# Loads in the order of need, and five projection blocks ahead of the first output projection, in a sliding-attention and gated feed-forward layer

## The chip, the core and the metric

One core of one Trainium2 chip runs the whole layer in one launch. The metric is the device time of that launch in microseconds (us). The kernel before took 820.35 us, the median of seven runs (820.05 to 825.86, six of them within 820.05 to 820.52). An edit is judged by the ratio of its time to this kernel's on the same chip.

## What is computed

The input is x, 2048 rows of 1024 bf16 numbers. The layer adds a dilated sliding attention and then a gated feed-forward to it, each behind a layer norm.

```python
qkv = layernorm(x) @ wqkv                      # 1024 -> 3 x 1024, 32 heads of 32
off = arange(8) * 2                            # a row sees 8 rows: itself, 2, 4, ... 14 back
logits = einsum("bhsd,bhswd->bhsw", q, kg) * 32 ** -0.5
attn = softmax(where(mask, logits, -1e9))
h = x + einsum("bhsw,bhswd->bhsd", attn, vg) @ wo
g, u = layernorm(h) @ w_gate, layernorm(h) @ w_up      # 1024 -> 3584 each
out = h + (g * u) @ w_down
```

## The kernel before, in words

**Tiling.** The 2048 rows are worked in four chunks of 512. A chunk's normalized rows lie transposed in SBUF as lnT (three buffers), so that TensorE can use them as the moving operand. Weights stream through a pool of seven buffers of 1 MB, one for each block of 512 columns. The query-key-value projection of a chunk has six such blocks (two for queries, two for keys, two for values) of four groups of eight 128x512 matmuls; ScalarE evicts each group from PSUM (L249) and SP stores it to DRAM (L252 for queries, L261 for keys and values), from where Pool's DMAs fetch it back with heads and quarter-chunks on the partitions (L351, L352, L357), the layout in which VectorE does the attention. The result goes through DRAM again (L427, L430) into oT, for the output projection with wo, its residual add and the second layer norm (`wo_ln2`, L440 to L467). Then come the gate and up projections (`ffn1`) and the down projection (`ffn2`).

**Order of TensorE's work.** Chunk 0's projection, chunk 1's, chunk 2's, four blocks of chunk 3's, the output projection of chunk 0, the last two blocks of chunk 3's, and then for each chunk `ffn1`, the next chunk's `wo_ln2`, `ffn2` (L528 to L550). The first block of chunk 0 is a stage of its own, the opening: as each quarter of 128 rows arrives, VectorE takes its statistics and normalizes it, TensorE transposes it into PSUM (`first_transpose`, L285), ScalarE copies half of the transposed tile to SBUF and VectorE the other half (`first_copy`, L291), and TensorE multiplies it with block 0 of wqkv (`first_mm`, L294).

**Order of the rest.** The program order of every engine is written out by hand. `Background` (L33) holds generators: the first layer norm of chunks 1 to 3 (`ln1`, L188) and the attention of each chunk (`attention`, L364). After each group of matmuls `bg.step` lets them emit as much VectorE work as the group's 1.73 us pay for. An engine runs its instructions in that order, so where a wait stands in an engine's queue, all that was emitted later on it stands behind.

**The opening loads.** SP issues, in this order: quarters 0 and 1 of x, block 0 of wqkv in two halves, quarter 2, block 1 of wqkv in two halves, quarter 3 (L221, L213), and then with `pump` (L144) blocks 2 to 5 of wqkv and the first block of wo (L148). Pool copies one element of quarter 3 (L320), which makes it wait for that load, and then issues the loads of x for chunks 1 to 3 (L182). Each DMA that SP issues takes the next of eight semaphores, and waits until the DMA that used it before, eight places earlier, has landed.

**Buffers that tie stages together.** Eight buffers hold quarters of x or h, so the loads of chunk 2 wait for chunk 0's normalizing and those of chunk 3 for chunk 1's. Four buffers (`ln`) hold normalized quarters until their DMA transpose (L196, L447) has landed. PSUM has eight buffers, and 30 buffers (`t1k`) hold evicted groups.

Of the kernel before, what the change touches and what calls it, by code (L numbers as in the profile page):

```python
# [8 lines left out]
BF = mybir.dt.bfloat16  # L9
# [14 lines left out]
TC = 512  # L24
NCH = S // TC
SUB = TC // 4
KO = D // 128
# [48 lines left out]
def kernel(  # L76
# [11 lines left out]
    nc = tc.nc  # L88
# [50 lines left out]
        for b in range(4):  # L139
            stream.append((("wd", NCH - 1, hf, b), wd_v[:, bass.ts(b, 7), bass.ts(hf, 512)], 7))  # L140
    wts = {}
    state = {"next": 0, "live": 0}

    def pump(eng=None):  # L144
        while state["next"] < len(stream) and state["live"] < 7:
            key, src, n = stream[state["next"]]
            wt = wpool.tile([128, KO, 512], BF, tag="w", name="w_" + "_".join(map(str, key)))
            (eng or nc.sync).dma_start(wt[:, 0:n, :], src)  # L148
            wts[key] = wt
            state["next"] += 1  # L150
            state["live"] += 1

# [25 lines left out]
    def load_x(c, what, eng):  # L178
        tiles = []
        for t in range(4):  # L180
            xt = hp.tile([128, D], BF, tag="h", name=f"{what}{c}_{t}")
            eng.dma_start(xt[:], x[bass.ds(c * TC + t * 128, 128), :])  # L182
            tiles.append(xt)
        return tiles

    lnTs = {}

    def ln1(c):  # L188
        xts = load_x(c, "x", nc.gpsimd)
        yield "later", 8.0 if c < 3 else 5.0  # L190
        lnTs[c] = lnTp.tile([128, KO, TC], BF, tag="lnT", name=f"lnT1_{c}")
        mv4, rs4 = ln_tiles(f"1_{c}")

        def norm(t):
            ln = normalize(xts[t], mv4, rs4, t)
            nc.sync.dma_start_transpose(lnTs[c][:, :, bass.ts(t, 128)], ln[:])  # L196

        for t in range(4):
            stats(xts[t], mv4, t)
            rstd_of(mv4, rs4, t, t + 1)  # L200
            yield 1.5
            if t > 0:
                norm(t - 1)
                yield 0.55
        norm(3)
        yield 0.55


    def load_w(parts=1):
        key, src, n = stream[state["next"]]  # L210
        wt = wpool.tile([128, KO, 512], BF, tag="w", name="w_" + "_".join(map(str, key)))
        for q in range(parts):
            nc.sync.dma_start(wt[:, bass.ts(q, KO // parts), :], src[:, bass.ts(q, KO // parts), :])  # L213
        wts[key] = wt
        state["next"] += 1
        state["live"] += 1

    x0 = [hp.tile([128, D], BF, tag="h", name=f"x0_{t}") for t in range(4)]

    def load_x0(t):  # L220
        nc.sync.dma_start(x0[t][:], x[bass.ds(t * 128, 128), :])  # L221

    load_x0(0)
    load_x0(1)
    load_w(2)
    load_x0(2)
    load_w(2)
    load_x0(3)
    nc.scalar.preload_act_table_set("natural_log_exp_and_others")
    warm = const.tile([128, 512], BF)  # L230
# [52 lines left out]
        lns[t] = normalize(x0[t], mv0, rs0, t)  # L283

    def first_transpose(t):  # L285
        pts[t] = psum.tile([128, KO, 128], BF, tag="mm", name=f"pt{t}")
        for kk in range(KO):
            nc.tensor.transpose(pts[t][:, kk, :], lns[t][:, bass.ts(kk, 128)], ident[:])  # L288
        nc.scalar.copy(lnTs[0][:, 0:4, bass.ts(t, 128)], pts[t][:, 0:4, :])  # L289

    def first_copy(t):  # L291
        nc.vector.tensor_copy(lnTs[0][:, 4:8, bass.ts(t, 128)], pts[t][:, 4:8, :])  # L292

    def first_mm(t, kos):  # L294
        for ko in kos:
# [20 lines left out]
        if t < 3:  # L316
            first_rstd(t + 1)
    first_mm(3, range(8))
    order_after_x0 = const.tile([128, 1], BF)
    nc.gpsimd.tensor_copy(order_after_x0[:], x0[3][:, 0:1])  # L320
    pump()
    bg.add(ln1(1))
    bg.add(ln1(2))
    for j in range(4):
# [35 lines left out]
    def prefetch_qk(c):  # L360
        if c in stored and ("q", c) not in qkv_in:
            load_qk(c)

    def attention(c):  # L364
        if c == 0:
            load_qk(0)
            load_v(0)
            yield "later", 7.0
        qD, kD, vD = qkv_in["q", c], qkv_in["k", c], qkv_in["v", c]
        lg = att.tile([128, W, SUB], F32, tag="lg", name=f"lg{c}")  # L370
        for wp in range(W // 2):
            prod = att.tile([128, 2, DH, SUB], BF, tag="prod", name=f"prod{c}_{wp}")
            for j in range(2):
                o = HB - DIL * (2 * wp + j)
                nc.vector.tensor_tensor(prod[:, j], qD[:], kD[:, :, o:o + SUB], ALU.mult)  # L375
                yield 2.3
            nc.vector.tensor_tensor(prod[:, :, 0:16], prod[:, :, 0:16], prod[:, :, 16:32], ALU.add)  # L377
            yield 2.3
            nc.vector.tensor_tensor(prod[:, :, 0:8], prod[:, :, 0:8], prod[:, :, 8:16], ALU.add)
            yield 1.2  # L380
            t3 = att.tile([128, 2, 4, SUB], F32, tag="t3", name=f"t3{c}_{wp}")
            nc.vector.tensor_tensor(t3[:], prod[:, :, 0:4], prod[:, :, 4:8], ALU.add)
            yield 1.2
            nc.vector.tensor_tensor(t3[:, :, 0:2], t3[:, :, 0:2], t3[:, :, 2:4], ALU.add)
            nc.vector.tensor_tensor(lg[:, 2 * wp:2 * wp + 2, :], t3[:, :, 0], t3[:, :, 1], ALU.add)
            yield 1.0
        if c == 0:
            nc.vector.tensor_tensor(lg[0:32, :, 0:16], lg[0:32, :, 0:16], mask[:], ALU.add)
        tr = att.tile([128, 4, SUB], F32, tag="t3", name=f"tr{c}")
        nc.vector.tensor_tensor(tr[:], lg[:, 0:4], lg[:, 4:8], ALU.max)  # L390
        nc.vector.tensor_tensor(tr[:, 0:2], tr[:, 0:2], tr[:, 2:4], ALU.max)
        mx = att.tile([128, SUB], F32, tag="mx", name=f"mx{c}")
        nc.vector.tensor_tensor(mx[:], tr[:, 0], tr[:, 1], ALU.max)
        nc.vector.tensor_tensor(lg[:], lg[:], mx[:, None, :].to_broadcast((128, W, SUB)), ALU.subtract)
        nc.scalar.activation(lg[:], lg[:], ACTF.Exp, scale=float(DH) ** -0.5)
        yield 3.5
        tr2 = att.tile([128, 4, SUB], F32, tag="t3", name=f"trs{c}")
        nc.vector.tensor_tensor(tr2[:], lg[:, 0:4], lg[:, 4:8], ALU.add)
        nc.vector.tensor_tensor(tr2[:, 0:2], tr2[:, 0:2], tr2[:, 2:4], ALU.add)
        sm = att.tile([128, SUB], F32, tag="mx", name=f"sm{c}")  # L400
        nc.vector.tensor_tensor(sm[:], tr2[:, 0], tr2[:, 1], ALU.add)
        rs = att.tile([128, SUB], F32, tag="rs", name=f"rs{c}")
        nc.vector.reciprocal(rs[:], sm[:])
        yield 2.5
        prefetch_qk(c + 1)
        at = att.tile([128, W, SUB], BF, tag="at", name=f"at{c}")
        nc.vector.tensor_tensor(at[:], lg[:], rs[:, None, :].to_broadcast((128, W, SUB)), ALU.mult)
        yield 1.2
        oD = att.tile([128, DH, SUB], BF, tag="oD", name=f"oD{c}")
        for wp in range(W // 2):  # L410
            pv = att.tile([128, 2, DH, SUB], BF, tag="prod", name=f"pv{c}_{wp}")
            for j in range(2):
                w = 2 * wp + j
                o = HB - DIL * w
                nc.vector.tensor_tensor(pv[:, j], vD[:, :, o:o + SUB],  # L415
                                        at[:, w, None, :].to_broadcast((128, DH, SUB)), ALU.mult)
                yield 2.3
            prefetch_qk(c + 1)
            if wp == 0:
                nc.vector.tensor_tensor(oD[:], pv[:, 0], pv[:, 1], ALU.add)  # L420
                yield 2.3
            else:
                nc.vector.tensor_tensor(pv[:, 0], pv[:, 0], pv[:, 1], ALU.add)  # L423
                yield 2.3
                nc.vector.tensor_tensor(oD[:], oD[:], pv[:, 0], ALU.add)  # L425
                yield 2.3
        nc.gpsimd.dma_start(od[c].rearrange("c g d s -> (c g) d s"), oD[:])  # L427
        oT = att.tile([128, KO, 4, SUB], BF, tag="oT", name=f"oT{c}")
        for cp in range(4):
            nc.gpsimd.dma_start(oT[:, :, cp, :], od[c][cp].rearrange("(hg hl) d s -> (hl d) hg s", hl=4))  # L430
        oTs[c] = oT
        while c + 1 < NCH and ("q", c + 1) not in qkv_in:
            yield "later", 1.0
            prefetch_qk(c + 1)
        if c + 1 < NCH:
            load_v(c + 1)
# [86 lines left out]
    def start_attention(c):  # L523
        stored.add(c)
        atts[c] = attention(c)
        bg.add(atts[c], bg.now + (5.0 if c == 0 else 0.0))

    qkv(0, range(1, 6))  # L528
    bg.add(ln1(3))
    start_attention(0)  # L530
    qkv(1, range(6))
    start_attention(1)
    qkv(2, range(6))
    start_attention(2)
    hss[0] = load_x(0, "h", nc.sync)
    qkv(3, range(4), last=True)
    bg.finish(atts[0])
    bg.rate = 0.9
    nxt = wo_ln2(0)
    qkv(3, range(4, 6), last=True)  # L540
    start_attention(3)
    for c in range(NCH):
        lnT2, hs = nxt
# [35 lines left out]
```

## Time and profile before

| | |
|---|---|
| time, median of seven runs | 820.35 us |
| the profiled execution: its own time, and its span | 820.75 us, 819.0 us |
| TensorE busy | 806.1 us of the span |
| VectorE, ScalarE, Pool busy | 470.6, 222.5, 31.2 us |
| TensorE's first group after the opening starts | 21.09 us |
| first output projection: first and last matmul | 166.13 us, about 180 us |
| first gate matmul of `ffn1` | 193.75 us |
| DMA traffic | 158.98 MB, mean 194 GB/s |

Times inside the span count from its first instruction. In lines of the timeline the columns are the start, the duration, the engine, the source line, the operation, output and inputs by the program's names, the number of instructions merged into the line, and in brackets how long the engine was idle before and what ended that wait. DVE is VectorE, ACT ScalarE, POOL GpSimd, PE TensorE's matmuls and PEld its weight loads. SPq is SP's queue, whose durations include what an issue waited for.

### The profile page before, as it was taken

What the parts mean: (1) busy time and instruction counts of PE and PEld (TensorE: products, weight loads), DVE (VectorE), ACT (ScalarE), POOL (GpSimd) and SP (SyncE); (2) the same over time, 40 slices, a digit from 0 to 9 for tenths busy, and PEclk for the clock granted to TensorE, in tenths of its full rate; (3) what the DMA queues carried; (4) which work ended last, traced back from release to release, by engine and by line L of the source; (5) the groups of instructions that cost most, each with busy time, mean ns of one, the idle gap of its engine ahead of it and who ended that gap; (6) DMA issues with size and microseconds to landing.
All of it is one profiled execution on the core that took longest, in us unless ns stands there. A gap on an engine that the chain in (4) does not pass through costs nothing.

```text
span 819.0 us, 9732 instructions
## 1 busy us (share of the span) xinstructions
PE 806.1 (98%) x3808; PEld 373.5 (46%) x3881; DVE 470.6 (57%) x520; ACT 222.5 (27%) x505; POOL 31.2 (4%) x60
## 2 busy tenths in 40 slices
PE   7999999999999999999999999999999999999998
PEld 4444444444444444444444444444444444444445
DVE  4538999998888999968887995111124111111011
ACT  2554444314333310023333000333320003333100
POOL 3100000200000200000100002000000000000000
PEclk9999999999999999999999999999999999999999
DMA  9999764999845879755863588736455763535400
GB/s 312 291 238 243 144 190 109 261 275 264 289 141 161 279 186 295 250 162 185 274 219 119 128 263 270 210 105 202 150 180 155 231 188 127 184 118 167 148 26 26
DMA packets 194494, 158.98 MB, mean 194 GB/s; under 512 B 83472, under 2 KB 188048, under 8 KB 192400
## 3 DMA queue, kind: packets, MB, share of 16 engines
q1 hardware_dynamic: 189904, 133.19, 57.1%
q0 software_dynamic: 4544, 25.17, 9.2%
q8 instruction: 30, 0.49, 0.2%
q14 instruction: 16, 0.13, 0.1%
HBM read 128.97 MB, written 22.02 MB: 184 GB/s over the span
## 4 chain that ended last, share of the span: by engine, by line
PE 97%; DMA 1%; issue 1%; SPq 0%; DVE 0%; ACT 0%
PE pg L330 24%; PE pu L330 23%; PE acc L512 21%; PE ps L330 19%; PE wo L453 7%; PE accl L502 3%; DMA x<-in_A_x_dram 1%; SPq L213 0%; PE ps L297 0%; SPq L221 0%; PE pt L288 0%; ACT lnT L289 0%; DVE ln L170 0%; DVE h L493 0%; DVE lnT L292 0%
## 5 line engine op out<-in xcount | busy, mean ns | idle before, releaser
L330 PE MATMUL pg<-lnT,w_wg 128*128 128x512 bf16 x879 | 210.1, 379 | 0.9
L330 PE MATMUL pu<-lnT,w_wu 128*128 128x512 bf16 x877 | 209.8, 379 | 0.9
L512 PE MATMUL acc<-w_wd,gs 128*128 128x512 bf16 x768 | 169.0, 379 | 0.8
L484 DVE TENSOR_TENSOR gs<-gs,us 128x512 bf16<-128x512 bf16 x112 | 47.4, 423 | 198.7 <-ACT us L483 198.7
L330 PE MATMUL ps<-lnT,w_qkv 128*128 128x512 bf16 x721 | 158.4, 379 | 0.8
L330 PEld LDWEIGHTS <-w_wg 128*128 128x128 bf16 x896 | 87.7, 98 | 105.7
L330 PEld LDWEIGHTS <-w_wu 128*128 128x128 bf16 x896 | 87.7, 98 | 105.7
L478 ACT CAST gs<-pg 128x512 bf16<-128x512 f32 x112 | 65.6, 586 | 235.9 <-PE pg L330 230.2
L512 PEld LDWEIGHTS <-gs 128*128 128x128 bf16 x784 | 76.8, 98 | 92.5
L330 PEld LDWEIGHTS <-w_qkv 128*128 128x128 bf16 x736 | 71.9, 98 | 86.6
L483 ACT CAST us<-pu 128x512 bf16<-128x512 f32 x112 | 65.6, 586 | 123.8 <-PE pu L330 114.6
L249 ACT CAST sg<-ps 128x512 bf16<-128x512 f32 x96 | 55.5, 586 | 64.6 <-PE ps L330 59.5
L415 DVE TENSOR_TENSOR pv<-vD,at 128x4096 bf16<-128x4096 bf16 x32 | 72.4, 2287 | 0.4
L375 DVE TENSOR_TENSOR prod<-qD,kD 128x4096 bf16<-128x4096 bf16 x32 | 72.3, 2285 | 0.1
L493 DVE TENSOR_TENSOR h<-acc,h 128x512 bf16<-128x512 f32 x28 | 17.4, 684 | 78.4 <-PE acc L512 78.4
L453 PE MATMUL wo<-w_wo,oT 128*128 128x512 bf16 x251 | 55.6, 379 | 0.3
L453 PEld LDWEIGHTS <-oT 128*128 128x128 bf16 x256 | 25.0, 98 | 30.2
L377 DVE TENSOR_TENSOR prod<-prod 128x4096 bf16<-128x4096 bf16 x16 | 36.6, 2289 | 0.3
L165 ACT ACTIVATE rs<-mv,eps 128x1 f32<-128x1 f32 x32 | 9.4, 294 | 75.0 <-DVE mv L162 69.9
L423 DVE TENSOR_TENSOR pv<-pv 128x4096 bf16<-128x4096 bf16 x12 | 27.5, 2289 | 0.2
L425 DVE TENSOR_TENSOR oD<-oD,pv 128x4096 bf16<-128x4096 bf16 x12 | 27.5, 2288 | 0.2
L502 PE MATMUL accl<-w_wd,gs 128*128 128x512 bf16 (+1 forms) x139 | 24.4, 336 | 0.1
(56 smaller groups left out, 291.0 us busy)
## 6 DMA issues: line engine op xcount, KB each, us to landing
w_wg<-in_B_w_gate_dram SPq DMA_DIRECT2D x28, 1024.0 KB, 7.2
w_wu<-in_B_w_up_dram SPq DMA_DIRECT2D x28, 1024.0 KB, 5.5
w_wd<-in_B_w_down_dram SPq DMA_DIRECT2D x32, 896.0 KB, 6.0
w_wo<-in_A_wo_dram SPq DMA_DIRECT2D x8, 1024.0 KB, 7.0
kd<-sg SPq DMA_DIRECT2D x32, 144.0 KB, 3.4
vd<-sg SPq DMA_DIRECT2D x32, 144.0 KB, 3.8
kD<-kd POOLq DMA_DIRECT2D x4, 1152.0 KB, 7.5
vD<-vd POOLq DMA_DIRECT2D x4, 1152.0 KB, 11.6
```

The lines of the kernel that those rows point to most:

```text
L249: nc.scalar.copy(sg[:, HB:HB + TC], ps[:])
L330: nc.tensor.matmul(ps[:], lhsT=wt[:, ko, bass.ts(j, 128)], rhs=rhs[:, ko, :], start=(ko == 0), stop=(ko == KO - 1))
L375: nc.vector.tensor_tensor(prod[:, j], qD[:], kD[:, :, o:o + SUB], ALU.mult)
L377: nc.vector.tensor_tensor(prod[:, :, 0:16], prod[:, :, 0:16], prod[:, :, 16:32], ALU.add)
L415: nc.vector.tensor_tensor(pv[:, j], vD[:, :, o:o + SUB], at[:, w, None, :].to_broadcast((128, DH, SUB)), ALU.mult)
L423: nc.vector.tensor_tensor(pv[:, 0], pv[:, 0], pv[:, 1], ALU.add)
L453: nc.tensor.matmul(ps[:], lhsT=oTs[c][:, kk, t, :], rhs=wts["wo", c, hf][:, kk, :], start=(kk == 0), stop=(kk == KO - 1))
L478: nc.scalar.copy(gs[:], pg[:])
L483: nc.scalar.copy(us[:], pu[:])
L484: nc.vector.tensor_tensor(gs[:], gs[:], us[:], ALU.mult)
L502: nc.tensor.matmul(acc[:], lhsT=hT[f][:, bass.ts(t, 128)], rhs=wts["wd", c, hf, f // 7][:, f % 7, bass.ds(lo, n)], start=(f == 0), stop=(f ...
L512: nc.tensor.matmul(acc[t][:], lhsT=hT[f][:, bass.ts(t, 128)], rhs=wts["wd", c, hf, b][:, j, :], start=(f == 0), stop=(f == NF - 1))
```

## The change

- **Loads.** Block 0 of wqkv is one tile loaded in two halves, the first ahead of quarter 2 of x, the second between quarters 2 and 3. Block 1 comes after all of x's chunk 0: Pool writes one element of its buffer after reading quarter 3, and SP's load waits for that. Then SP issues x of chunk 1, block 2, x of chunk 2, blocks 3 to 5; x of chunk 3 is loaded by SP too, at the start of `ln1(2)`. The first block of wo is loaded only after chunk 1's projection.
- **Opening.** The transposed quarter is split over two PSUM tiles, one for ScalarE's copy and one for VectorE's.
- **Chunk 3's norm.** Its four transposes are issued together after chunk 0's projection has been emitted, and not one by one.
- **Attention of chunk 0.** The fetch of q and k is emitted after block 3, when the keys are complete, that of v after block 5, and `attention` waits for v only where it uses it.
- **Five blocks.** Five blocks of chunk 3's projection, not four, stand ahead of the first output projection; one, not two, follows it.

```diff
-    def pump(eng=None):
-        while state["next"] < len(stream) and state["live"] < 7:
+    def pump(limit=None, wt=None):
+        state["limit"] = limit or state["limit"]
+        while state["next"] < state["limit"] and state["live"] < 7:
...
     def ln1(c):
-        xts = load_x(c, "x", nc.gpsimd)
-        yield "later", 8.0 if c < 3 else 5.0
+        if c == 2:
+            xtiles[3] = load_x(3, "x", nc.sync)
+        xts = xtiles[c]
...
+            if c < 3:
+                transpose(t)
...
+        if c == 3:
+            while "qkv0" not in emitted:
+                yield "later", 1.0
+            for t in range(4):
+                transpose(t)
...
     load_x0(0)
     load_x0(1)
-    load_w(2)
+    load_w0(0, 4)
     load_x0(2)
-    load_w(2)
+    load_w0(4, 4)
     load_x0(3)
...
     def first_transpose(t):
-        pts[t] = psum.tile([128, KO, 128], BF, tag="mm", name=f"pt{t}")
-        for kk in range(KO):
-            nc.tensor.transpose(pts[t][:, kk, :], lns[t][:, bass.ts(kk, 128)], ident[:])
-        nc.scalar.copy(lnTs[0][:, 0:4, bass.ts(t, 128)], pts[t][:, 0:4, :])
+        for hf in range(2):
+            pt = psum.tile([128, KO // 2, 128], BF, tag="mm", name=f"pt{t}_{hf}")
+            for kk in range(KO // 2):
+                nc.tensor.transpose(pt[:, kk, :], lns[t][:, bass.ts(4 * hf + kk, 128)], ident[:])
+            pts[t, hf] = pt
+        nc.scalar.copy(lnTs[0][:, 0:4, bass.ts(t, 128)], pts[t, 0][:])
...
-    order_after_x0 = const.tile([128, 1], BF)
-    nc.gpsimd.tensor_copy(order_after_x0[:], x0[3][:, 0:1])
-    pump()
+    w1 = wpool.tile([128, KO, 512], BF, tag="w", name="w_qkv_1")
+    nc.gpsimd.tensor_copy(w1[:, 0, 0:1], x0[3][:, 0:1])
+    pump(2, w1)
+    xtiles[1] = load_x(1, "x", nc.sync)
+    pump(3)
+    xtiles[2] = load_x(2, "x", nc.sync)
+    pump(6)
...
-        bg.add(atts[c], bg.now + (5.0 if c == 0 else 0.0))
+        bg.add(atts[c], bg.now + (27.0 if c == 0 else 0.0))
 
-    qkv(0, range(1, 6))
+    qkv(0, range(1, 4))
     bg.add(ln1(3))
+    load_qk(0)
     start_attention(0)
+    qkv(0, range(4, 6))
+    emitted.add("qkv0")
+    load_v(0)
     qkv(1, range(6))
     start_attention(1)
+    pump(len(stream))
     qkv(2, range(6))
     start_attention(2)
     hss[0] = load_x(0, "h", nc.sync)
-    qkv(3, range(4), last=True)
+    qkv(3, range(5), last=True)
     bg.finish(atts[0])
     bg.rate = 0.9
     nxt = wo_ln2(0)
-    qkv(3, range(4, 6), last=True)
+    qkv(3, range(5, 6), last=True)
```

## Prediction

> **What bounds the kernel now.** I read the page first: busy times and the chain that ended last.
>
> ```profile
> PE 806.1 (98%) x3808; PEld 373.5 (46%) x3881; DVE 470.6 (57%) x520; ACT 222.5 (27%) x505; POOL 31.2 (4%) x60
> PE 97%; DMA 1%; issue 1%; SPq 0%; DVE 0%; ACT 0%
> ```
>
> TensorE is the bound nearly throughout. TensorE's own waits all lie in the opening, before 21.09 us; from there to the end it never waits. So the change can gain only in the opening, and loses by every wait that it opens later. Next the timeline of the opening:
>
> ```profile
> 10.12 0.69 DVE L274 BATCH_NORM_STATS2 st<-x 128x6 f32<-128x512 bf16 x1 [1.94 <-DMA x<-in_A_x_dram]
> 13.79 0.69 DVE L274 BATCH_NORM_STATS2 st<-x 128x6 f32<-128x512 bf16 x1 [0.66 <-DMA x<-in_A_x_dram]
> 16.27 0.42 DVE L292 COPY lnT<-pt 128x512 bf16<-128x512 bf16 x1 [0.73 <-ACT lnT L289]
> 18.01 0.62 PE L288 MATMUL pt<-ident,ln 128*128 128x128 bf16 x8 [0.22 <-DVE ln L170]
> 21.09 1.24 PE L330 MATMUL ps<-lnT,w_qkv 128*128 128x512 bf16 x4
> ```
>
> Quarters 2 and 3 of x come at 10.12 and 13.79; the copy of half a quarter waits for ScalarE's; the opening ends at 21.09. The second place is the first output projection and what stands behind it:
>
> ```profile
> 57.97 0.53 POOL L352 DMA_DIRECT2D kD<-kd  x1 [16.04 <-DMA kd<-sg]
> 63.78 0.55 DVE L170 TENSOR_SCALAR ln<-x,mv,rs 128x1024 bf16<-128x1024 bf16 x1 [7.82 <-ACT rs L166]
> 68.68 4.49 DVE L375 TENSOR_TENSOR prod<-qD,kD 128x4096 bf16<-128x4096 bf16 x2
> 100.00:130.00 30.00, 29.84 (x138) 13.62 (x139) 28.19 (x24) 13.48 (x38) 1.06 (x2) 1.00 0.54 155
> 153.00:170.00 17.00, 16.95 (x79) 7.70 (x79) 16.79 (x10) 5.62 (x17) 4.63 (x6) 1.00 1.02 280
> 170.10 0.68 DVE L455 TENSOR_TENSOR h<-wo,h 128x512 bf16<-128x512 f32 x1
> 175.66 10.24 SPq L447 DMA_TRANSPOSE lnT<-ln  x4
> 193.75 1.89 PE L330 MATMUL pg<-lnT,w_wg 128*128 128x512 bf16 x7
> ```
>
> In the two lines of windows the fourth figure without brackets is VectorE's busy time. From 68.68 VectorE is busy without a gap over 1.2 us: it is late, and its first residual add runs at 170.10, though TensorE had the sum some 2 us earlier. The last transposed quarter lands at 187.80 in the trace, and `ffn1` needs it at 193.75: 5.95 us of slack, because two projection blocks (13.8 us) lie between.
>
> [...]
>
> **Opening.** In the new order the queue up to the first half of block 0 is as before, 7.90. Quarter 2 is next, 8.63; the second half 10.10 (0.73 later than before); quarter 3 10.84 (2.94 earlier, 1 MB less ahead). TensorE's first ko 4 and 5 wait for 10.10, then eight matmuls at 0.056 end at 10.59. Transposes of quarter 1: 10.6 (11.32 before). ScalarE's copy can start after four transposes, at 11.03, 0.59 long; the multiplication of quarter 1 starts at 11.67, 24 matmuls end at 13.0. VectorE's copy runs beside ScalarE's, so the norm of quarter 2 ends at about 12.94 and its transposes start at 13.0. One more turn takes 2.4: transposes, copy until 14.02, 24 matmuls until 15.40, while the chain copy 14.08, mean 14.2, ScalarE 14.77, norm 15.36 is just as long. The last turn: 15.41, copy until 16.43, 32 matmuls in 1.76. The opening ends at 18.24: 2.85 us gained. Block 1's load starts at about 11.14 (quarter 3, then Pool's 0.19 copy); 1 MB took 5.1 to 5.7 us in quiet stretches, so it lands at 16.4, 1.8 us before need. The rest follows at 2.94 per MB: x to 19.3, block 2 22.3 (needed 25.1), x 25.2, block 3 28.1 (needed 32.1), 31.1, 34.05. Nothing waits.
>
> **Chunk 0's attention.** It starts when keys are back: the last key store, 0.6 us to Pool's issue, 7.2 us for the fetch (57.97 to 65.18). The DMA engines are the limit there: the windows from 36 to 56 us show a busy share of 1.03 to 1.58. From the landing of the last opening block (35.23) to that of the last key store (57.35) 22.1 us passed with 16 stores, five transposes, 1 MB of x and the fetch of q. In the changed program's order SP has the same before the last key store, and three more transposes (all four of chunk 2). A transpose and a key store landed together every 1.45 to 1.74 us, a store alone 0.68; so a transpose is 0.95 and three are 2.85. The last key store lands at 34.05 + 22.1 + 2.85 = 59.0, the keys at 66.8, and attention starts at T = 66.9 and not 68.68. Low bound 64.0, if the three fit into gaps that the queue had (share 0.71 at 32 to 36); high 69.5, if SP's eight semaphores add another round of 2.6 (a transpose waiting behind the fetch of q). ScalarE's norms of chunk 3 now stand between evictions and wait for chunk 2's transposes (about 52.5), which puts an eviction at 55, where TensorE needs its PSUM buffer at 54.5: 0 to 1.5 us, hidden by the later wait below, or, without that, lost.
>
> **Five blocks.** TensorE reaches the first output projection at W = 18.24 + 22 x 6.907 = 170.2 (6.907 a block: 21.09 to 166.13 is 21), ends it at 184.0 and block 5 at 190.9. VectorE's order is what decides. Before, it needed 101.4 us from 68.68 to the first residual add at 170.10. In the changed order the add stands behind 8.1 us more of chunk 1's attention (1.26 + 1.26 + 0.72 + 0.34 + 4.52 from the rows between 159.79 and 167.89): T + 109.5 = 176.4, when TensorE had the sum at 172.1. From there one product-sum (2.2) and an add (0.6) to the second add, and from it to the last landing 15.96 as before (171.84 to 187.80): T + 128.3 = 195.2. `ffn1` could start at 190.9 and starts at 195.25, 4.3 us idle; before it started at 193.75. All later work is TensorE's, unchanged, so the end moves by T - 65.4 = **+1.5 us**: the 2.85 gained are lost again at `ffn1`, with some more, since only one block covers the norm. With T under 62.6 VectorE would be in time, the landing W + 20.76 against a need at W + 20.73, and the whole 2.85 would stay. [...]
>
> Free edits: the deferred transposes of chunk 3 (needed at 135), x on SP's queue (before, Pool's), the later wo block (needed 65 us after its issue), all covered by TensorE's projections; bare, a 1 MB load would be 5.5 us.
>
> **Sum.** Own time of the profiled run 820.75 (span 819.0) - 2.85 + 4.35 = 822.25; it stands 0.4 above the median of 820.35, so **821.9**. A measurement of this kernel can tell about 0.3% (2.5 us) from no change.
>
> **Rivals.**
> - *Lost at ffn1, clock kept* (forecast): T from 63 to 67.8, 818.0 to 822.8, likeliest 821.9. For it: VectorE's gapless run. Chance 0.52.
> - *Late keys* (slower): SP may issue a DMA only when the one eight places earlier has landed; if a transpose of chunk 1 lands behind the fetch of q, all later key stores wait for it, one more round of 2.6 us. Then T = 69.5 and 820.35 + 69.5 - 65.4 = 824.5. It decides from T = 67.9 on. For it: x of chunk 3 now stands in SP's queue ahead of these stores, and the fetch of q is not held behind it; against: the stores start no later than before. Chance 0.20.
> - [...] Chance 0.16.
> - *Gain kept* (faster): the keys are back before 62.6, VectorE is in time, 820.35 - 2.85 + 0.1 = 817.6. For it: q is fetched earlier, and the transposes may fit into gaps; against: equal DMA work. Chance 0.12.
>
> **How the numbers follow.** Faster is the last case, same the first, slower the two between. The range leaves out most of the last case and what lies beyond the late keys: 818.8 to 824.6; the likeliest's own is 820.4 (T = 65.4) to 822.8.
>
> **What would show it.** Quarter 3's statistics near 10.9; first L330 group at 18.2; VectorE's first L375 at 66.9; first residual add at 176.4; the last transpose landing at 195.2 and TensorE idle for 4 us ahead of its first gate matmul; no wait of TensorE after that. If the first product starts before 63 us, or the gate matmul at 191, I am wrong.

## The result, and the profile after

The changed kernel took 827.15 us (median of 24 runs, 823.49 to 829.82), against 820.33 for the kernel before: a ratio of 1.0069, 95% interval 1.0053 to 1.0085. It is slower, and lies above the forecast range of 818.8 to 824.6. Ratios compare means, to which the kernel before brings eight executions of 825.9 to 830.7 us out of 59 (one of 1071 us is left out), so they come out smaller than the quotients of the medians. The profiled execution took 825.13 us, with a span of 823.4.

The busy times, and the shares of the chain that ended last:

```profile
PE 807.5 (98%) x3808; PEld 374.0 (45%) x3881; DVE 471.2 (57%) x520; ACT 221.9 (27%) x505; POOL 24.6 (3%) x48
PE 79%; DVE 16%; DMA 4%; issue 1%; ACT 1%; SPq 0%; DVEq 0%
```

TensorE has the same instructions as before, but the chain no longer runs through it alone: 20% of the span now lies with VectorE and with transfers. The timeline of the opening shows the gain:

```profile
7.43 0.64 DVE L290 BATCH_NORM_STATS2 st<-x 128x6 f32<-128x512 bf16 x1
9.83 0.64 DVE L290 BATCH_NORM_STATS2 st<-x 128x6 f32<-128x512 bf16 x1
11.77 0.42 DVE L310 COPY lnT<-pt 128x512 bf16<-128x512 bf16 x1
16.37 1.89 PE L352 MATMUL ps<-lnT,w_qkv 128*128 128x512 bf16 x7
```

The statistics of quarters 2 and 3 (7.43 and 9.83) wait for nothing, VectorE's copy no longer waits for ScalarE's (11.77 to 12.19, beside ScalarE's from 11.55 to 12.14; in the kernel before it waited 0.73 us for it, at 16.27), and the opening ends at 16.37 us, 4.72 earlier than before. All of that and more is lost at two waits, and by a clock that fell in one of them. The list of TensorE's waits gives the time, the count and the longest:

```profile
PE pg L352 <- DMA lnT<-ln: 5.0, 1, 5.0
PE ps L352 <- ACT halo L273: 2.0, 1, 2.0
```

The timeline shows what the long one stands behind:

```profile
60.34 0.55 POOL L374 DMA_DIRECT2D kD<-kd  x1 [20.26 <-DMA vd<-sg]
67.98 2.29 DVE L393 TENSOR_TENSOR prod<-qD,kD 128x4096 bf16<-128x4096 bf16 x1 [8.62 <-DMA kD<-kd]
177.52 0.68 DVE L476 TENSOR_TENSOR h<-wo,h 128x512 bf16<-128x512 f32 x1
183.61 10.77 SPq L468 DMA_TRANSPOSE lnT<-ln  x4
184.40 7.07 PE L352 MATMUL ps<-lnT,w_qkv 128*128 128x512 bf16 x32
196.42 0.58 PE L352 MATMUL pg<-lnT,w_wg 128*128 128x512 bf16 x1 [4.96 <-DMA lnT<-ln]
```

VectorE is idle for 8.62 us until the keys are back at 67.9, starts attention at T = 67.98 (68.68 before, although the opening now ends 4.7 us sooner), and comes to the first residual add at 177.52 (170.10 before). The last of the four transposes lands at 196.28. TensorE has finished its one covering block at 191.46. The windows around the wait have, after PE, PEld, DVE, ACT and POOL, the granted clock, the DMA share and GB/s:

```profile
191.40:193.00 1.60, 0.07 (x1) 0.00 (x0) 0.97 (x3) 0.95 (x4) 0.00 (x0) 1.00 0.73 135
193.00:196.40 3.40, 0.00 (x0) 0.01 (x1) 3.30 (x5) 1.89 (x8) 0.00 (x0) 0.57 0.60 95
196.40:199.80 3.40, 3.16 (x8) 1.17 (x10) 2.50 (x2) 0.00 (x0) 0.00 (x0) 0.50 1.03 350
199.80:203.00 3.20, 3.20 (x15) 1.46 (x14) 0.40 (x2) 1.17 (x2) 0.00 (x0) 0.92 1.12 332
```

The clock falls to half inside the wait, at about 193.5 us, and stays there until about 200.3: the first eight gate matmuls take 3.4 us and not 1.73. `ffn1` starts 2.67 us later than before (193.75 then) and loses 1.7 by the clock: 4.37, and the two profiled executions differ by 825.13 - 820.75 = 4.38.

### The profile page after: what moved, and what is told of

Its sections match the earlier page's. It is cut to its first block, busy times and chain, and to the rows that moved or that the text cites. A ratio compares the mean times of both kernels' runs of the same rounds, so it can differ in the third digit from the quotient of the medians.

```text
span 823.4 us, 9716 instructions
## 1 busy us (share of the span) xinstructions
PE 807.5 (98%) x3808; PEld 374.0 (45%) x3881; DVE 471.2 (57%) x520; ACT 221.9 (27%) x505; POOL 24.6 (3%) x48
## 4 chain that ended last, share of the span: by engine, by line
PE 79%; DVE 16%; DMA 4%; issue 1%; ACT 1%; SPq 0%; DVEq 0%
PE pg L352 24%; PE pu L352 23%; PE acc L533 20%; PE wo L474 5%; DVE prod L393 4%; PE accl L523 3%; DVE pv L436 2%; DVE prod L395 2%; DMA lnT<-ln 2%; PE ps L352 1%; DVE st L164 1%; PE ps L315 1%; DMA kD<-kd 1%; DVE prod L397 1%; DVE t L400 1%; DVE pv L444 1%
## 5 line engine op out<-in xcount | busy, mean ns | idle before, releaser
L474 PE MATMUL wo<-w_wo,oT 128*128 128x512 bf16 x251 | 55.6, 379 | 0.3
```

Source lines behind the costliest of these rows:

```text
L474: nc.tensor.matmul(ps[:], lhsT=oTs[c][:, kk, t, :], rhs=wts["wo", c, hf][:, kk, :], start=(kk == 0), stop=(kk == KO - 1))
```

## The experiments

My theory ahead of the runs was that the fifth block costs the time, by VectorE's place in its own order; the first rival was that the new loads cost it. T is the start of chunk 0's attention on VectorE, "opening" the start of TensorE's first group after it. A join is a place where TensorE first needs a result of VectorE's attention: the output projection, and behind it `ffn1`. Opening, T and the start of `ffn1` come from one profiled execution of each kernel, the times and ratios (to the kernel before) from the timed runs. Where a median and a trace differ, only the trace shows causes.

| run | time, us | ratio (95% interval) | opening | T | ffn1 starts |
|---|---|---|---|---|---|
| changed kernel | 827.15 | 1.0069 (1.0053 to 1.0085) | 16.37 | 67.98 | 196.42 |
| e_four | 825.82 | 1.0058 (1.0043 to 1.0073) | 17.99 | 70.58 | 200.13 |
| e_five_only | 821.63 | 1.0022 (1.0002 to 1.0041) | 20.39 | 67.98 | 194.31 |
| e_hold | 820.28 | 0.9987 (0.9970 to 1.0004) | 16.73 | 67.98 | 192.23 |
| e_warm | 824.92 | 1.0052 (1.0032 to 1.0072) | 17.43 | 70.31 | 198.82 |
| e_light | 818.61 | 0.9963 (0.9945 to 0.9982) | 16.69 | 64.82 | 193.29 |
| e_ln3 | 824.91 | 1.0036 (1.0016 to 1.0057) | 17.31 | 67.58 | 196.02 |
| e_hold_ln3 | 816.84 | 0.9938 (0.9913 to 0.9962) | 17.62 | 67.63 | 190.47 |
| e_open_only | 825.50 | 1.0047 (1.0028 to 1.0066) | 17.36 | 69.44 | 194.51 |
| e_x3_pool | 829.60 | 1.0105 (1.0067 to 1.0143) | 17.43 | 75.00 | 203.42 |
| e_four_ln3 | 822.47 | 1.0008 (0.9988 to 1.0028) | 17.18 | 67.22 | 195.96 |
| e_before_late | 827.12 | 1.0070 (1.0047 to 1.0093) | 21.10 | 73.21 | 199.58 |
| e_no_x3 | 823.09 | 1.0015 (0.9994 to 1.0035) | 17.24 | 66.31 | 194.70 |
| e_k_first | 826.92 | 1.0061 (1.0035 to 1.0087) | 17.09 | 69.64 | 198.09 |

**1. e_four: the loads alone.**

```diff
-    qkv(3, range(5), last=True)
+    qkv(3, range(4), last=True)
...
-    qkv(3, range(5, 6), last=True)
+    qkv(3, range(4, 6), last=True)
```

> The changed kernel with four blocks of chunk 3's projection ahead of the first output projection again; loads and opening stay as changed. Theory (the fifth block costs the time, as it puts 8.1 us more of attention ahead of the first residual add and leaves one block of cover behind it): TensorE gets to the output projection at 163.7, waits up to 3 us there for the attention's result, and two blocks then cover the norm, so no wait at ffn1: 820.5 to 821.5 us, ratio to the kernel before 1.000 to 1.0015. Rival (the new order of loads itself costs the time: the keys come 2.6 us later and ScalarE holds an eviction up): as slow as the changed kernel, 825 to 827 us, with the same wait ahead of the first gate matmul.

It took 825.82 us. My theory, as I had put it, fell: without the fifth block nearly all the loss is there. But the rival's wait at `ffn1` isn't there either. Its timeline and its windows show the place:

```profile
169.60 16.87 PE L474 MATMUL wo<-w_wo,oT 128*128 128x512 bf16 x63 [3.88 <-DMA oT<-od]
```

```profile
170.00:175.00 5.00, 5.00 (x13) 1.81 (x12) 4.97 (x4) 0.00 (x0) 0.00 (x0) 0.50 1.05 342
```

With four blocks TensorE comes to the output projection itself too early, waits there for chunk 0's attention, and runs it in 16.87 us and not 13.98, since the clock is at half. The same late attention is met at another join. So the theory that the further runs tested is: T starts a gapless run of VectorE, and TensorE's lead is lost wherever it first needs a result of that run.

**2. e_five_only: the fifth block alone.** In the kernel before:

```diff
-    qkv(3, range(4), last=True)
+    qkv(3, range(5), last=True)
...
-    qkv(3, range(4, 6), last=True)
+    qkv(3, range(5, 6), last=True)
```

> The kernel before with one edit, five blocks and not four ahead of the first output projection; loads and opening as before. Theory: attention starts at 68.7 as before, the first residual add moves from 170.1 to 178.2, the last transposed quarter from 187.8 to about 196, TensorE is ready at 193.75 and waits 2 to 3.3 us, perhaps with a halved clock after it: 822.5 to 825 us, ratio 1.003 to 1.006. Rival (the loads cost the time): 820.3 us, ratio 1.000, no wait at ffn1.

821.63 us, less than expected: T was 67.98 and not 68.68, so the last quarter landed at 194.07 and TensorE waited 1.1 us, with no halved clock after it. The fifth block alone costs a little, the loads alone more, and each for want of VectorE's result.

**3. e_hold: VectorE's order held during the fifth block.**

```diff
-    qkv(3, range(5), last=True)
+    qkv(3, range(4), last=True)
+    bg.rate = bg.credit = 0.0
+    qkv(3, range(4, 5), last=True)
...
+        bg.rate = 1.0 if c == 0 else 0.9
         hT = ffn1(c, lnT2)
```

> The changed kernel with five blocks, but no attention of chunk 1 is emitted during the fifth block; it is made up for during the gate and up projections. VectorE then comes to the first residual add at 169.4 and not 177.5, before TensorE has the sum. Theory (VectorE's place in its own order is the loss): last transposed quarter at about 190.5, the first gate matmul at 191.5, no wait and no halved clock: 817.5 to 818.5 us, ratio 0.9965 to 0.998. Rival (what TensorE does or loads late is the loss, whatever stands in VectorE's order): 825 to 827 us as before this edit. Rival (the deferred attention then makes the second output projection late): no wait at the first gate matmul, but a new one near 290 us, and 820 us or more.

820.28 us, 6.9 less than the changed kernel: about the 5.0 us of wait and the 1.7 of clock. The loads and T are those of the changed kernel, and now VectorE waits for TensorE at the first residual add, and the first gate matmul starts without a wait:

```profile
173.18 0.69 DVE L476 TENSOR_TENSOR h<-wo,h 128x512 bf16<-128x512 f32 x1 [2.43 <-PE wo L474]
192.23 1.89 PE L352 MATMUL pg<-lnT,w_wg 128*128 128x512 bf16 x7
```

VectorE's place in its own order is shown to be the loss at `ffn1`; the second rival's wait near 290 us did not come. In this trace the hold was just enough: the last quarter landed at 192.09 us, and TensorE was ready at 192.13. The time was still 2 us above my figure, and the run's own waits told where to look next, since this one is now a cost in full:

```profile
PE ps L352 <- ACT halo L273: 2.3, 1, 2.3
```

**4. e_warm: the wait filled with matmuls.**

```diff
     qkv(3, range(5, 6), last=True)
+    keep = psum.tile([128, 512], F32, tag="mm", name="keep_ps")
+    for i in range(20):
+        nc.tensor.matmul(keep[:], lhsT=warm[:, 0:128], rhs=warm[:], start=True, stop=True)
```

> The changed kernel with 20 matmuls of 128x512 on zeros into a spare PSUM buffer between the last projection block and the first gate matmul (4.3 us of TensorE in a wait of about 5 us); their result is not used. Theory (the halved clock is a separate cost after the wait): the first gate group runs at full clock, 1.6 us less than the changed kernel, 825.5 us or a ratio 0.998 to it, mean clock 0.999. Rival (the clock was not lowered by the wait): no difference to the changed kernel.

824.92 us, 2.2 less than the changed kernel, with the first gate group in 1.89 us. The clock is a cost of its own behind the wait. Its trace has another drop that I had not looked for, after the wait for ScalarE near 54 us, here 2.6 us long (clock 0.63 in this line of its windows):

```profile
58.40:62.00 3.60, 3.60 (x12) 1.32 (x11) 0.55 (x1) 3.47 (x14) 0.00 (x0) 0.63 0.89 206
```

**5. e_light: 2 MB fewer ahead of the keys.**

```diff
-    pump(6)
+    pump(4)
...
-                mm_group(ps, wts["qkv", b], j, lnTs[c])
+                mm_group(ps, wts["qkv", min(b, 3) if c == 0 else b], j, lnTs[c])
...
     load_v(0)
+    pump(6)
     qkv(1, range(6))
```

> The changed kernel, but blocks 4 and 5 of wqkv are loaded only after chunk 0's stores; chunk 0's values are computed with block 3's weights in their place, so that part of the computation is changed, in the same time. 2 MB fewer pass the DMA engines ahead of the last key store. Theory (attention starts when the DMA traffic ahead of the key stores is through, and that start T sets the rest): T falls by up to 5.9 us (2 x 2.94), from 68 to 62-64; the last transposed quarter lands at T + 128.3 = 190.3 to 192.3, TensorE is ready at about 190, the wait at ffn1 is under 2 us and the clock stays up: 818 to 820 us, ratio 0.997 to 1.000. Rival (SP's order and its waits on VectorE set T, not the bytes): T stays near 68 and the time near 826 us.

818.61 us: T depends on the DMA traffic ahead of the key stores, and with an earlier T the time comes back, with nothing changed at the output projection. (Bytes, and places in SP's queue, are not told apart: the two loads take both.) T came 48.1 us after the opening, where the four traces of programs that are alike until then (changed kernel, e_four, e_hold, e_warm) have 51.3 to 52.9. So 2 MB are worth some 4 us here and not the 5.9 that I took. In 17 of its 22 executions the mean clock was 1.000, at 818.5 us on average. The traced one, 821.79, was not among them and still waited:

```profile
193.29 2.64 PE L352 MATMUL pg<-lnT,w_wg 128*128 128x512 bf16 x8 [3.77 <-DMA lnT<-ln]
```

**6. e_ln3: chunk 3's norm out of ScalarE's way.**

```diff
-    bg.add(ln1(3))
+    bg.add(ln1(3), bg.now + 8.6)
```

> The changed kernel with the first layer norm of chunk 3 emitted five groups (8.6 us) later, so that its Ln and Exp no longer stand between ScalarE's evictions at 48 to 54 us. Theory (T bounds what follows, so an earlier TensorE only waits longer at ffn1): the wait of 2.0 us near 54 us goes, T stays within 0.7 us, the wait at ffn1 grows by as much: 826 to 827.5 us, at best 1.7 less where the clock was halved near 54 us. Rival (the held-up eviction is a cost of its own): 824.5 to 825 us.

824.91 us: the rival's figure. The wait for ScalarE is gone, and TensorE waits 5.9 us at `ffn1`, more than the 5.0 of the changed kernel, though not by the whole 2.0 us of my theory; T came 50.3 us after the opening and not 51.3 to 52.9. With the norm later, the last key store lands 42.1 us after the opening and not 43.3 to 44.1, and that is why TensorE's freed time did not all go into the next wait. Why the stores land sooner these runs don't show.

**7. e_hold_ln3: both.** The edits of runs 3 and 6 together.

> The run with VectorE's order held during the fifth block, and with chunk 3's norm five groups later besides. Theory (even then T bounds: the attention's result lands at T + 105 when TensorE reaches the output projection): within 0.7 us of the run with the hold alone, 819.5 to 820.5 us, with a new short wait at the output projection. Rival (TensorE is the bound there, so its earlier time counts): 2 us less, 818 to 818.5 us.

816.84 us, the best kernel here: 0.9938 of the kernel before, and 10.3 us less than the changed kernel. My theory fell again, for the reason of run 6: T moved, by 2 us against the alike traces (50.0 after the opening). The shares of its chain and its timeline show TensorE as the bound from the opening on:

```profile
PE 98%; DMA 1%; SPq 0%; DVE 0%; issue 0%
```

```profile
169.57 13.98 PE L474 MATMUL wo<-w_wo,oT 128*128 128x512 bf16 x64
183.38 7.07 PE L352 MATMUL ps<-lnT,w_qkv 128*128 128x512 bf16 x32
190.47 1.89 PE L352 MATMUL pg<-lnT,w_wg 128*128 128x512 bf16 x8
```

No wait, no halved clock, and the opening's gain is kept to the last: 21.09 - 17.62 = 3.47, and 820.75 - 3.47 = 817.28 is what this execution took.

**8. e_open_only: the opening alone.** In the kernel before, the loads of block 0 and x in the new order, block 1 behind Pool's copy, and the two PSUM tiles:

```diff
-    load_w(2)
+    load_w0(0, 4)
     load_x0(2)
-    load_w(2)
+    load_w0(4, 4)
     load_x0(3)
...
-    order_after_x0 = const.tile([128, 1], BF)
-    nc.gpsimd.tensor_copy(order_after_x0[:], x0[3][:, 0:1])
+    w1 = wpool.tile([128, KO, 512], BF, tag="w", name="w_qkv_1")
+    nc.gpsimd.tensor_copy(w1[:, 0, 0:1], x0[3][:, 0:1])
+    nc.sync.dma_start(w1[:], wqkv_v[:, :, 512:1024])
...
     pump()
```

> The kernel before with the opening alone changed: order of block 0's halves, x and block 1, and two PSUM tiles for a transposed quarter; x of the later chunks stays on Pool, the first block of wo early, the norm of chunk 3 and the attention of chunk 0 as before, four blocks ahead of the output projection. Theory: the opening ends 2.9 to 4.7 us earlier; in the kernel before 5.95 us of slack lie between the norm's landing and ffn1, so as long as attention starts no later than 70 us the gain stays: 816 to 818 us, ratio 0.995 to 0.997. Rival (any earlier opening is lost, since attention starts by DMA traffic and TensorE then waits at the output projection): 820 us, ratio 1.000, with a wait of 2 to 4 us at the output projection or ffn1.

825.50 us, so I was wrong by far: an earlier opening alone makes this kernel slower. Timeline and windows of its trace (an execution of 821.08 us):

```profile
24.89 27.80 PE L344 MATMUL ps<-lnT,w_qkv 128*128 128x512 bf16 x128 [0.46 <-DMA w_qkv<-in_A_wqkv_dram]
54.70 112.35 PE L344 MATMUL ps<-lnT,w_qkv 128*128 128x512 bf16 x512 [2.01 <-ACT halo L265]
```

```profile
54.00:58.00 4.00, 3.30 (x11) 1.40 (x12) 3.31 (x7) 3.84 (x16) 0.00 (x0) 0.73 1.47 201
58.00:62.00 4.00, 4.00 (x18) 1.64 (x16) 0.00 (x0) 3.33 (x12) 0.54 (x1) 0.84 0.95 169
```

Of 3.73 us gained, 0.46 go to a block that comes late, 2.01 to ScalarE's evictions, and the two windows below full clock cost 4 x 0.27 + 4 x 0.16 = 1.7. The rival named the wrong places but the right kind: what TensorE gains ahead of a chain that did not get faster, it waits for. Where the other 4.4 us of the median lie is open, as only this execution, the fastest of 22, was traced. The clock is a part of it: the mean clock was 0.998 in eleven executions (824.1 us on average) and 0.996 in eight (826.8); but two at 1.000 took 822.9 as well, longer than the kernel before.

**9. e_x3_pool: x of chunk 3 on Pool's queue again.**

```diff
-            xtiles[3] = load_x(3, "x", nc.sync)
+            xtiles[3] = load_x(3, "x", nc.gpsimd)
```

> The changed kernel with the four loads of x for chunk 3 on Pool's queue again and not in SP's. Theory (SP's queue is held up by these loads: a transpose issued behind them took 5.16 us, and six of the eight key stores stand behind it): the last key store comes 1.5 to 3 us earlier after the opening than the 43.3 us of the changed kernel, T likewise, and the time falls by as much: 824 to 825.5 us. Rival (the bytes ahead of the stores decide, on whichever queue): T and time as in the changed kernel, 826.5 to 827.5 us.

829.60 us: neither. T went to 75.0. The view of its DMA queues for 40 to 60 us (packets, MB and share of a queue; KB and us to landing of an issue) and one of its windows:

```profile
q1 hardware_dynamic: 8326, 2.14, 74.3%
q0 software_dynamic: 144, 1.05, 35.0%
...
qD<-qd POOLq DMA_DIRECT2D x1, 1024.0 KB, 13.6
```

```profile
46.00:48.00 2.00, 2.00 (x10) 0.91 (x10) 0.10 (x1) 1.94 (x8) 0.00 (x0) 1.00 0.51 29
```

The four loads did land early, but then the next transposes were issued into the fetch of q, which took 13.6 us; in the changed kernel it took 7.0. The engines moved 29 GB/s in this window, so it isn't bytes that filled the time. A transpose issued at 43.24 landed at 56.96, and seven key stores after that. TensorE itself waited 4.1 us for chunk 1's rows and 3.5 for ScalarE, and its clock was halved from 55.6 to 69.3 us. What stalled is open; that the queue in which loads stand can cost more than their bytes is shown.

**10. e_four_ln3: four blocks, with ScalarE free.** The edits of runs 1 and 6 together.

> The changed kernel with four blocks ahead of the first output projection and with chunk 3's first norm five groups later, so that no eviction waits behind it. Theory (attention's start T bounds this kernel too, now at the output projection): TensorE is ready at 162.5 to 164, the first piece of the attention's result lands at T + 99 = 166.5 to 167.5, a wait of 3 to 4 us and perhaps a halved clock: 821.5 to 823.5 us. Rival (once no eviction is held up, four blocks are enough): 817 to 818 us, no wait at the output projection.

```profile
166.63 15.67 PE L474 MATMUL wo<-w_wo,oT 128*128 128x512 bf16 x63 [4.25 <-DMA oT<-od]
```

822.47 us, as the theory had it: a wait of 4.25 us, and 1.69 for the clock (15.67 - 13.98). Against e_hold_ln3 the same loads and the same norm differ by the fifth block and the hold alone: 5.6 us. So the fifth block is worth having, if VectorE's order is made to fit it. (No run has the hold with four blocks.)

**11. e_before_late: attention started later in the kernel before.**

```diff
     def attention(c):
...
+        if c == 0:
+            spare = att.tile([128, 2, DH, SUB], BF, tag="prod", name="spare")
+            for j in range(2):
+                nc.vector.tensor_tensor(spare[:, j], qD[:], kD[:, :, HB:HB + SUB], ALU.mult)
```

> The kernel before with two more products of q and k (4.58 us of VectorE, their result is not used) ahead of chunk 0's attention; nothing else is changed. Theory (attention's start is nearly the bound in the kernel before already: the first piece of its result lands at 165.0 and TensorE needs it at 166.13): a wait of 3.5 us at the output projection, 823.8 us, or 825.5 us with a halved clock for one window behind it. Rival (the kernel before has 5.95 us of slack, the one ahead of ffn1): 820.3 us, no wait.

```profile
170.26 15.67 PE L457 MATMUL wo<-w_wo,oT 128*128 128x512 bf16 x63 [3.95 <-DMA oT<-od]
```

827.12 us: the theory, at its upper end and 1.6 over. In the traced execution T rose by 4.53, the first piece of the attention's result landed 5.20 later (165.01, 170.21), the output projection starts 4.13 later and runs 1.69 longer: 5.82, and the execution took 826.57 - 820.75 = 5.82 more. The kernel before ran with 1.1 us of slack at this join.

**12. e_no_x3: without the loads of x for chunk 3.**

```diff
-            xtiles[3] = load_x(3, "x", nc.sync)
+            xtiles[3] = xtiles[2]
```

> The changed kernel without the loads of x for chunk 3: its norm reads chunk 2's rows again, so that part of the result is changed, and 1 MB less is loaded. Theory (in SP's queue these four loads stand between the fetch of q and six key stores, and land from 47.0 to 49.1 us, 0.7 us apart): the last key store lands 2.2 to 2.8 us earlier after the opening than the 43.3 us of the changed kernel, T likewise, 824 to 825 us. Rival (what made the run with these loads on Pool slow: without them the next transposes are issued into the fetch of q, and this fetch takes 13.6 us and not 7): T at 72 to 75 us, 828.5 to 830 us.

823.09 us, and T 49.1 us after the opening (51.3 to 52.9 in the alike traces); the last key store landed 41.8 us after it (43.3 to 44.1). This is the theory's side, a little beyond it. The fetch of q took 7.6 us, so what made run 9 slow isn't the missing loads as such.

**13. e_k_first: k fetched before q.**

```diff
         nc.gpsimd.dma_start(kD[:], kd[c].rearrange("c g d s -> (c g) d s"))
+        nc.gpsimd.dma_start(qD[:], qd[c].rearrange("c g d s -> (c g) d s"))
```

(the line of q is moved from above that of k)

> The changed kernel with Pool fetching k before q for each chunk, so that no fetch runs beside chunk 0's transposes and key stores. Theory (the fetch of q, 7 us of all DMA engines, stands ahead of the key stores, but has to be made before attention in any case): the last key store lands 4 to 7 us earlier, at 53 to 56 us, then k and q follow for 7 us each: T = 67 to 70 us, the time within 1.5 us of the changed kernel. Rival (the fetch hinders the transposes beyond its own 7 us): T at 64 to 66 us, 823 to 825 us.

826.92 us, as with q first. The last key store lands at 58.65 us, 41.6 after the opening, some 2 us sooner and not 4 to 7; then k is back at 66.58 and q at 69.54. The time is the theory's: what moving the fetch of q away from the key stores gains, the fetch costs behind them.

## Why the prediction was wrong, point by point

**Right: the mechanism and its place.** Forecast was that the opening's gain is lost at `ffn1`, through VectorE's gapless run from T. The constant of that run is the best number of the prediction: T + 128.35 was forecast for the first gate matmul. In the six traces that wait there with five blocks and no hold (changed kernel, e_warm, e_light, e_ln3, e_no_x3, e_k_first) it starts at T + 128.39 to T + 128.51, for T from 64.8 to 70.3. Right, too, were the first residual add at T + 109.5 (109.54), and that no weight of these blocks is waited for. The number failed by two terms: the clock, for which the sum has no term, cost 1.70 us, and T came 1.08 us later than forecast.

**T: "attention starts at T = 66.9".** It was 67.98, and in the three other programs that are alike until then 67.98, 70.31 and 70.58. The terms of the sum, as forecast and in the trace: last opening block landed 34.05, 32.55; from there to the last key store 24.95, 27.1 (59.67 - 32.55); from there to attention 7.9, 8.3. So the step that failed in T is "22.1 us passed" plus "three are 2.85": it lacks 2.2 us. I had counted that the window held 1 MB of x before and after, and not where in the queue: before, these loads came ahead of the fetch of q on Pool; now they stand behind it in SP's queue and ahead of seven key stores, and land from 46.97 to 49.13, after the fetch (46.34) and before the stores (49.85 on). Without them (run 12) the last key store is 1.5 to 2.3 us earlier. But that run takes their bytes away too, and with the loads back on Pool's queue (run 9) T came later still, so that it is their place which makes the 2.2 us is argued and not shown.

**The opening: "2.85 us gained".** 4.72 in the trace, and 3.1 to 4.4 in the alike programs. The first half of block 0 landed at 5.71 us in the changed kernel, and at 7.74, 6.14 and 7.21 in the three others; I had taken 7.90 from the one trace of the kernel before. The rates of the sum are those of the kernel before, whose opening loads landed in order of issue at 7.90, 9.37, 10.10, 11.58, 13.06 and 13.77 (0.71 to 0.73 us per 256 KB, 1.47 to 1.48 per 512 KB), and they held: 5.71, 6.40, 7.89 and 8.54 in the changed kernel, 0.65 to 0.69 and 1.49, and later 2.85 to 3.03 per 1 MB block. The size was wrong, and by luck this helped: T moves with the opening (51.3 to 52.9 us behind it) and the end with T, so that the opening's loads, 1.5 us sooner than forecast, hid most of the 2.2 us that the sum for T lacked. This may also be the spread of the changed kernel's times: with T from 68.0 to 70.6, 825.1 to 827.7 would follow, and the median would ask for T = 70. It is not shown, and the clock is a second candidate: ten of the 24 executions had a mean clock of 0.993 to 0.995 (827.9 us on average), nine the 0.996 of the traced one (826.3).

**The clock: no term in the sum.** The chance of 0.16 for a halved clock was my estimate, with no run behind it: the kernel before, where TensorE's longest wait is 1.3 us, keeps full clock until 818 us. Every traced wait of TensorE from 3.8 us on at these two joins came with a stretch of halved clock: changed kernel, e_light, e_ln3, e_no_x3 and e_k_first at `ffn1`, e_four, e_four_ln3 and e_before_late at the output projection, eight of eight, at 1.5 to 2.9 us each (from the first gate matmul to the end 624.8 to 625.2 us pass in the kernel before and where the clock stays up, 626.7 to 627.7 in these; the output projection takes 13.98, and here 15.67 to 16.87). The waits of 1.1 us (e_five_only) and 2.0 us (changed kernel) did not; those near 54 us of 2.0 (e_open_only) and 2.6 (e_warm) did, and of 2.2 (e_four) and 2.3 (e_hold) did not.

What decides can be worked out from the traces. In all of them the clock changes in steps of 3.41 us: a halved stretch in mid-kernel lasts 3.41, 6.83 or 13.65 us. Here are windows cut at these steps, two each from the changed kernel, e_hold and e_open_only. The length is followed by TensorE's busy time, and the granted clock is the last figure but two:

```profile
190.08:193.49 3.41, 1.39 (x7) 0.42 (x5) 2.78 (x6) 1.45 (x5) 0.00 (x0) 1.00 0.42 79
193.49:196.90 3.41, 0.48 (x1) 0.24 (x3) 3.31 (x5) 1.40 (x6) 0.00 (x0) 0.50 0.70 128
53.77:57.19 3.42, 1.76 (x8) 0.78 (x8) 2.48 (x7) 2.44 (x11) 0.00 (x0) 1.00 1.07 213
57.19:60.60 3.41, 3.41 (x17) 1.53 (x16) 0.55 (x1) 3.29 (x14) 0.00 (x0) 1.00 0.65 156
52.44:55.85 3.41, 1.40 (x8) 0.62 (x7) 2.55 (x7) 2.42 (x10) 0.00 (x0) 1.00 1.22 206
55.85:59.26 3.41, 3.41 (x10) 1.24 (x9) 2.01 (x5) 3.25 (x15) 0.00 (x0) 0.50 1.10 146
```

TensorE was idle for 2.02 us of the first window, and the next one is at half; for 1.66 us in e_hold, whose wait of 2.3 us is cut in two by a step, and the clock stays up; for 2.01 us in e_open_only, and the next one is at half. Over all 15 traces, the eleven windows at full clock that stand ahead of a fall have 2.01 to 3.41 us of idle time, and every other one has 1.73 us at most. So in these traces the clock fell behind every window with 2.01 us of idle time or more, and behind no other. In nine of the eleven TensorE had worked for a part of the window, so that a wholly idle one is not needed. A wait of 4 us puts some 2 us into one of two windows wherever the step falls; one of 2 to 3 us does so or not. The chance is the step that failed here: by these traces a halved clock was the case to forecast at 4.3 us of idle time, and not one of 0.16.

**ScalarE: "hidden by the later wait below, or, without that, lost".** The wait was 2.0 us (0 to 1.5 forecast). Hidden it was not wholly: run 6 gained 2.2 with five blocks unheld, by an earlier T, which I had not connected with it.

**Slack.** The prediction names 5.95 us of slack at `ffn1` and passes over the 1.1 us at the output projection (first piece of the attention's result landed at 165.01, first matmul at 166.13). Runs 1, 10 and 11 show that the second is the one that decides with four blocks.

**Sum.** 822.25 forecast for the profiled execution, + 1.08 for T, + 0.09 for the constant, + 1.70 for the clock = 825.12; it took 825.13. The median is 2.0 above that; a T as in the other traces (70.3, 70.6) would account for it, but no execution at the median was traced, so this part stays open.

## What to carry to other kernels

Before you price an earlier start of the bound engine, list every place where it first needs another engine's result, with the slack at each, and work out whether that engine starts earlier too: here two joins with 1.1 and 5.95 us took a gain of 4.7. If work of the bound engine is moved ahead of such a join, the order written for the other engine must be moved with it, or it fills the time with work that isn't due. And price a wait of TensorE of some 4 us at its length and another 1.7 us for the clock (1.5 to 2.9 here).

## What the runs showed of the hardware that was not expected

- The landing of the same load in the same queue position is not a constant: the first half of block 0 landed at 5.71 to 7.74 us in the four alike programs.
- What SP issued beside a 1 MB fetch by Pool landed after it. In the changed kernel the fetch of q was issued at 39.39 and landed at 46.34; the loads of x issued from 40.35 on landed from 46.97, and the key stores issued at 42.86 and 43.35 at 49.85 and 50.52, 7.0 and 7.2 us after their issue, where the next three (49.17, 51.14, 53.11) took 2.4 to 2.7. In run 9 q landed at 57.17, the next store at 57.62. In the view of run 9 Pool's 144 packets are 7.3 KB each, SP's 8326 are 257 bytes each; whether the sizes make the delay is not shown. The fetch isn't all of it: with q's fetch out of the stores' way (run 13) the last one came only some 2 us sooner. Why the fetch of run 9 took 13.6 us, with 29 GB/s in one of its windows, is open.
- The issue of one transpose took 5.16 us in SP's queue (43.92 in the changed kernel) and 10.54 in run 9, where its neighbours took 1.25 to 1.34; its input was ready and its semaphore free, and what it waits for is open.
